# Softmax weights of a two-layer cached decode: from one permuting product and a VectorE turn to 32 small products and a ScalarE copy

## The chip, the cores and the metric

The kernel runs on one core of a Trainium2 chip. The metric is the device time of one launch in microseconds (us). Three runs of the kernel before the change took 235.09, 235.81 and 235.82 us; their median is 235.81 us. A profile was taken of one further execution, which took 235.61 us.

## The reference: what is computed

Two equal layers act on one token for each of eight batch rows (B = 8, D = 448): attention over a cache, then a small two-matrix network, each with a residual. Only the last 1024 of the 4096 cache positions are used. There are 16 query heads of 256 numbers and 8 cache heads, so two query heads share each cache head.

```python
q = (norm(x) @ wq) as 16 heads of 256
scores = q . k / 16          # per head, over W = 1024 positions
p = softmax(scores)
o = p . v
x = x + o @ wo               # 4096 -> 448
x = x + silu(norm(x) @ w1) @ w2     # 448 -> 1792 -> 448
# all of it twice; both layers use the same weights and the same cache
```

The cache dominates the memory traffic: for one batch row, 8 key slices and 8 value slices of 512 KB each, 67 MB for all eight rows. Each slice is loaded once and serves both layers.

## The kernel before, in words

**Batch rows as a pipeline.** The eight batch rows b = 0 to 7 go through the core one after the other, two of them at a time: while row b is in layer two, row b+1 is in layer one. A period of this pipeline holds, by the names that the kernel gives to its steps:

- `chain(b)`: the path with little parallel work between layer one's attention and layer two's scores: `fold1`, `xb1` (the new x in columns), `stat1`, `w1`, `yT`, `tanh`, `hT`, `w2`, `rowb2`, `fold2`, `xb2`, `x2b`, `stat2`, `wq0`/`wq1` (the new queries), `qT`, `qm`, `qd`, `qbd2`.
- scores: `S1.0` and `S1.1` (layer two of row b, key heads 0 to 3 and 4 to 7) and `S0.0`, `S0.1` (layer one of row b+1). Line 645. Each is four items of eight products; four quarters of TensorE's columns work on four key heads.
- `softmax(b, L)`, lines 654 to 676: VectorE finds the maximum (`max`, `mT`, `mg`, `mb`), ScalarE takes the exponential (`exp`, line 664), TensorE and VectorE bring the result into the form that the value products need (`perm`, line 666, and `turn`, line 668), and `l` with `rl` or `lc` makes the sums.
- values: `PVA` and `PVD` (layer one of row b+1, lines 709 and 728), `PV1.0` and `PV1.1` (layer two of row b, line 709), with ScalarE evictions `oevA.0`, `oevA.1`, `oevD`, `oev1` and small turning products `oT...`.
- `woA`, `woD` (line 781) and the eviction `rowb1` (line 1063), which feeds the next `fold1`.
- `KT0` to `KT7` (line 630): VectorE transposes each arriving key slice in its slot, two halves for each slice; a slice is scored only after that.
- `zero` (line 833): products with zeros, without use for the result.

**The change's place.** After `exp`, the exponentials E have (quarter, head) on the partitions and the 256 columns of a softmax tile in the free dimension. The value products want them the other way round, as columns of weights. Before, `perm` is one product with the constant matrix `perm` as weights and E as the moving operand (256 wide); VectorE's `turn` then transposes 32 x 32 blocks of the result into `pT_sb`.

**Loads.** SyncE issues all cache loads, in the order keys 0 to 7, values 0 to 7 for row 0, then row 1, and so on, into 30 slots used in a ring. Load n waits until load n-30 has been read for the last time. So values 6 and 7 of row b+1 wait for keys 0 and 1 of row b, which are last read by `S1.0` of row b; the keys of row b+2 wait for the rest of row b's keys and for its values. `wo` and `w2` are loaded behind row 0's keys, `w1` behind its values.

**Order.** Each task states what it reads and writes, and the program derives the waits. The order in which each engine takes its tasks is written out by hand: `ORDER` holds a string for each engine, one character for each task, which says how many of the engine's tasks not yet taken (in program order) are skipped. An engine takes its tasks strictly in that order, so a task that waits holds up everything behind it.

**Start.** VectorE's order begins with memsets of constants and of PSUM banks (`init`, `initb`, line 331), mixed with the first key transposes `KT0@0` and so on (the number behind @ is the batch row). `rsum` (lines 435 and 443) sums the columns of `w2` and `wo` on VectorE and in 20 pieces on ScalarE; `rsumd` writes the sums beside the weights, and `woD@0` needs all of those of `wo`.

Of the kernel before, what the change touches and what calls it, by code (L numbers as in the profile page):

```python
# [4 lines left out]
BF16 = mybir.dt.bfloat16  # L5
# [3 lines left out]
ACTF = mybir.ActivationFunctionType  # L9
# [5 lines left out]

ORDER = {
    "pe": (
        "000000011111l111133312223022051002010033300710500300111117777000440033333210011004403330201101044000"
        "1770000300111117777000400444423010011155510022011101044000177005000011111777700040044442320001115514"
        "0022201101044000177710000011111777700040044442320001161514002201110004400017716111101111177770004004"  # L20
        "4442320001161510022201110105400017771000001111177770004004444232000116151002201111010033001777710100"
        "ccc0b1111060000444442200011817771002022220000033ccc43a02060500001140333333300110000022220b1200000000"
        "11000"),
    "dve": (
        "pSG0G0bGq0njnwvZtutFtUEg4CQz0g4yBydzjhvHwbvnFrEAAzkayz352iuj9k6q935nikb8g14f2a4439nj90888c8685c09664"
        "4551122baaa2a929216bd1aaa10077700555555000010098880870705ac09a90087700555550000100098880870705ac09aa"
        "0077700555550000100a08880878060aab09a0087700555550000100098880870705aa0aa90077700555550000100a088808"
        "78060aab0990087700555550000100098880778060acb0b99a900005555500000000099ag90ebb8ba8006004403020100001"
        "111100000000"),
    "act": (  # L30
        "13333442444455f5e56432322224222111111113312211111111111331211111111111133122111111111113312211111111"
        "11133122100000000000220111000000000302011000000004002200010010000000"),
    "pool": (
        "00010011022002200200020002000010001000"),
}


# [164 lines left out]
def bass_interleave_layers__sliding_block_cached__dense_activation_silu__decode_kernel(  # L202
# [35 lines left out]
    perm = sb("perm", [P, P], BF16)  # L238
# [17 lines left out]
    pT_sb = [qbd[i][:, 8:264] for i in range(2)]  # L256
    E_sb = [qbd[i][:, 264:520] for i in range(2)]
# [23 lines left out]
    def QB(i, k2):  # L281
        return [("qbd", i, k2)]

    def bk(i):
        return [("bank", i)]
# [16 lines left out]
    def pe(fns, reads, writes, row, name):  # L302
        add("pe", fns, reads=reads, writes=writes, row=row, name=name)
# [63 lines left out]
    PERM = [("perm", 0), ("perm", 1)]  # L367
# [286 lines left out]
    def softmax(b, L):  # L654
        m, tb = mm[L], LB[L]
        x = bank[SC[L]][:, 0:256]
        l_ps = bank[SC[L]][:, 256:256 + H]
        dve(lambda e: e.tensor_reduce(m[:, 0:1], x, AX.X, ALU.max, negate=True), bk(SC[L]), [("mm", L)], b, "max%d" % L)  # L658
# [3 lines left out]
        dve(lambda e: e.transpose(m[:].rearrange("p (z n q) -> p z n q", z=2, q=4), view(mg[L][:], 0, [(0, 2), (1, 4), (0, 4)])),  # L662
            [("mg", L), ("mm", L)], [("mm", L)], b, "mb%d" % L)
        act(lambda e: e.activation(E_sb[L], x, ACTF.Exp, bias=m[:, 0:1], scale=1.0, accum_out=esum[:, L:L + 1]),  # L664
            bk(SC[L]) + [("mm", L)], QB(L, 1) + [("es", L)], b, "exp%d" % L)
        pe(lambda e: e.matmul(bank[tb][:, 0:256], perm[:], E_sb[L], start=True, stop=True),  # L666
           QB(L, 1) + PERM, bk(tb), b, "perm%d" % L)
        dve(lambda e: e.transpose(view(pT_sb[L], 0, [(64, 4), (1, 2), (2, 32)]),  # L668
                                  bank[tb][:, 0:256].bitcast(BF16)[:, 1:512:2].rearrange("p (u s n) -> p u s n", s=2, n=32)),
            bk(tb), QB(L, 0), b, "turn%d" % L)  # L670
# [459 lines left out]
```

## Time and profile before

| | |
|---|---|
| median of three runs | 235.81 us (235.09 to 235.82) |
| the profiled execution | 235.61 us, of which the span from first to last instruction is 233.7 us |
| busy: TensorE, VectorE, ScalarE, GpSimd | 168.2, 155.3, 68.5, 22.8 us |
| moved by DMA | 78.2 MB, nearly all in the first 35 of 40 slices |
| instructions | 8070 |

In the rows of the profile PE is TensorE (PEld its weight loads), DVE is VectorE, ACT is ScalarE, POOL is GpSimd, and SP is SyncE, which here only issues loads. A row of the timeline gives the start in us from the beginning of the span, the time it took, the engine, the line of the kernel, the operation, what it writes and reads, and how many instructions stand together in the row; in brackets stands how long the engine had been idle and what ended that. A row of a group of instructions gives the busy time, the mean duration of one in ns, and the idle time in front of them.

### The profile page before, as it was taken

How to read it: one execution, taken by the hardware profiler on the slowest of the kernel's cores; microseconds unless marked ns; L12 is line 12 of the kernel's file. 1: busy time of each engine (PE TensorE's matmuls, PEld its weight loads, DVE VectorE, ACT ScalarE, POOL GpSimd, SP SyncE). 2: the span in 40 equal slices, each digit the busy share in tenths (PEclk: the TensorE clock that was granted, in tenths of full speed). 3: DMA queues.
4: the chain of work that ended last, by engine and by line, in shares of the span. 5: the costliest groups of instructions: out<-in, count | busy, mean ns of one | idle time of the engine just before them, and what ended most of it. 6: DMA issues, size and time to landing. Idle time of an engine off the chain costs nothing.

```text
span 233.7 us, 8070 instructions
## 1 busy us (share of the span) xinstructions
PE 168.2 (72%) x3569; PEld 93.4 (40%) x3569; DVE 155.3 (66%) x412; ACT 68.5 (29%) x205; POOL 22.8 (10%) x42
## 2 busy tenths in 40 slices
PE   0001505488788888989788898889788987999873
PEld 0001503123454455446344543644464454456441
DVE  3038999986963896488578649955974795365501
ACT  2000002896222321331332233225213322333330
POOL 1000022000300200200012001101010110012000
PEclk9999999999999999999999999999999999999999
DMA  6999999999999999999999999999999998300000
GB/s 163 413 403 407 379 381 399 407 407 412 405 403 392 414 404 356 365 414 409 400 406 406 400 400 409 409 326 407 410 406 382 411 409 329 127 3 3 3 1 4
DMA packets 23401, 78.20 MB, mean 335 GB/s; under 512 B 3127, under 2 KB 6086, under 8 KB 22982
## 3 DMA queue, kind: packets, MB, share of 16 engines
q1 hardware_dynamic: 22806, 77.30, 84.7%
q8 instruction: 28, 0.46, 0.8%
q10 hardware_dynamic: 560, 0.38, 0.8%
q14 instruction: 7, 0.06, 0.1%
HBM read 77.67 MB, written 0.01 MB: 332 GB/s over the span
## 4 chain that ended last, share of the span: by engine, by line
PE 47%; DVE 22%; DMA 13%; ACT 10%; issue 5%; SPq 2%; ACTq 0%; DVEq 0%
DMA slot<-in_A_k_cache_dram 13%; PE bank L645 11%; DVE slot L630 9%; PE bank L709 7%; PE bank L872 6%; PE bank L781 4%; DVE slot L435 3%; PE bank L845 2%; ACT qbd L664 2%; PE bank L728 2%; PE bank L516 2%; ACT slot L443 2%; PE bank L885 2%; ACT qbd L698 1%; PE bank L666 1%
## 5 line engine op out<-in xcount | busy, mean ns | idle before, releaser
L630 DVE STREAM_TRANSPOSE slot<-slot 128x512 uint32<-128x512 uint32 x128 | 81.9, 682 | 16.6 <-DMA slot<-in_A_k_cache_dram 16.3
L645 PE MATMUL bank<-slot,qbd 128*16 128x256 bf16 (+1 forms) x1024 | 40.4, 286 | 7.0 <-ACT qbd L889 3.2
L645 PEld LDWEIGHTS bank<-slot,qbd 128*16 128x16 bf16 (+1 forms) x1024 | 23.9, 88 | 17.8 <-ACT qbd L889 7.2
L709 PE MATMUL bank<-slot,qbd 128*4 128x512 bf16 (+1 forms) x384 | 27.9, 388 | 1.8 <-DVE xb L584 1.3
L819 POOL TENSOR_TENSOR fcols<-fcols 128x1 f32<-128x1 f32 x17 | 9.4, 553 | 109.6 <-ACT fcols L817 109.6
L781 PE MATMUL bank<-wo_sb,q1s 128*1 128x449 bf16 x284 | 17.0, 362 | 0.4 <-ACT wo_sb L447 0.4
L872 PE MATMUL bank<-wq_sb,xbz 128*2 128x256 bf16 x512 | 16.7, 275 | 0.1
L833 PE MATMUL bank<-ident,cols 128*128 128x512 bf16 x48 | 16.2, 391 | 0.0
L620 POOL TENSOR_TENSOR qbd<-q1s,fcols 128x256 bf16<-128x256 bf16 x16 | 9.6, 612 | 65.1 <-PE bank L689 59.1
L889 ACT ACTIVATE qbd<-bank 128x256 bf16<-128x256 f32 x16 | 6.1, 383 | 32.9 <-PE bank L885 32.9
L668 DVE STREAM_TRANSPOSE qbd<-bank 128x256 bf16<-128x256 bf16 x16 | 7.7, 478 | 12.1 <-PE bank L666 11.5
L683 DVE TENSOR_TENSOR q1s<-bank,q1s 128x16 bf16<-128x16 f32 (+1 forms) x18 | 2.9, 160 | 17.7 <-PE bank L689 17.5
L698 ACT ACTIVATE qbd<-bank 128x256 bf16<-128x256 f32 x22 | 8.3, 382 | 18.4 <-PE bank L709 16.8
L709 PEld LDWEIGHTS bank<-slot,qbd 128*4 128x4 bf16 (+1 forms) x384 | 8.1, 84 | 12.6 <-issue 2.1
L536 DVE STREAM_TRANSPOSE bank<-bank 128x256 f32<-128x256 f32 (+1 forms) x25 | 10.8, 433 | 3.6 <-PE bank L1004 1.2
L872 PEld LDWEIGHTS bank<-wq_sb,xbz 128*2 128x2 bf16 x512 | 11.4, 82 | 2.8 <-DVE xbz L807 0.4
L549 PE MATMUL bank<-xb,cols 128*128 128x8 bf16 x4 | 0.3, 173 | 16.6 <-DVE cols L331 16.6
L703 ACT ACTIVATE qbd<-bank 128x512 bf16<-128x512 f32 x14 | 8.3, 595 | 11.8 <-PE bank L728 10.9
L728 PE MATMUL bank<-slot,qbd 128*12 128x512 bf16 (+3 forms) x124 | 11.2, 408 | 0.0
L658 DVE TENSOR_REDUCE mm<-bank 128x1 f32<-128x256 f32 x16 | 6.8, 423 | 6.1 <-PE bank L645 5.4
L443 ACT ACTIVATE slot<-w_sb 128x448 bf16<-128x448 bf16 x6 | 3.5, 576 | 22.3 <-DMA w_sb<-in_B_w_dram 22.2
L845 PE MATMUL bank<-w_sb,q1s 128*1 128x449 bf16 x98 | 6.5, 353 | 4.8 <-DVE q1s L827 4.8
(158 smaller groups left out, 229.9 us busy)
## 6 DMA issues: line engine op xcount, KB each, us to landing
slot<-in_A_k_cache_dram SPq DMA_DIRECT2D x64, 512.0 KB, 8.5
slot<-in_A_v_cache_dram SPq DMA_DIRECT2D x64, 512.0 KB, 11.0
wo_sb<-in_A_wo_dram SPq DMA_DIRECT2D x1, 3584.0 KB, 25.5
wq_sb<-in_A_wq_dram SPq DMA_DIRECT2D x3, 1024.0 KB, 8.7
w_sb<-in_B_w_dram SPq DMA_DIRECT2D x1, 1568.0 KB, 27.8
w_sb<-in_B_w_dram SPq DMA_DIRECT2D x1, 1344.0 KB, 17.6
wq_sb<-in_A_wq_dram SPq DMA_DIRECT2D x1, 256.0 KB, 3.6
wq_sb<-in_A_wq_dram ACTq DMA_DIRECT2D x1, 256.0 KB, 4.0
```

The costliest lines, as they stand in the source:

```text
L536: dve(lambda e: e.transpose(view(bank[bi][:], n, [(2, n // 32), (n // 16, 16), (1, 2)]), bank[bi][:, 0:n].rearrange("p (g r s) -> p g r s" ...
L620: pool(lambda e, k2=k2: e.tensor_tensor(qdata(0, k2), q1s[:, b, 64 * k2:64 * k2 + 64].rearrange("p (n r) -> p n r", r=2).unsqueeze(3) .bro ...
L630: dve(lambda e, v=v: e.transpose(v, v), SL(s, h), SL(s, h), b, "KT%d" % k)
L645: fns.append(lambda e, w=w, j=j, kv=kv, cb=cb, par=par: e.matmul(sc[32 * j:32 * j + up_to, 0:256], w, kv, start=(cb == 0 and par == 0), st ...
L698: act(lambda e, s=s: e.activation(E_sb[L], ob[:, s * DH:(s + 1) * DH], ACTF.Copy), bk(OB[L]), QB(L, 1), b, "oev%s.%d" % (name, s))
L709: return [lambda e, u=u: e.matmul(bank[OB[L] if ob is None else ob][32 * j:32 * j + 2 * n, :], pT_sb[L][:, pcol(u, c0):pcol(u, c0) + 2 * n ...
L728: pe([lambda e, t=t, c0=c0, w=w, kvh=kvh: e.matmul(bank[OB[0]][32 * t:32 * t + 2 * w, :], pT_sb[0][:, pcol(2 * t, c0):pcol(2 * t, c0) + 2 ...
L781: fns.append(lambda e, i=i, w=w, c0=c0: e.matmul(bank[XB][32 * (i % 4):32 * (i % 4) + 1, c0:c0 + D + 1], oT(i), w, start=(i < 4), stop=(i ...
L819: pool(lambda e: e.tensor_tensor(rhalf, var4, nhalf, ALU.pow), ["var4", "nhalf"], ["rhalf"], b, "pow" + name)
L833: pe(lambda e: e.matmul(bank[SC[1]][:, :], cols[:, 3:4].broadcast_to([P, P]), view(ident[:], 0, [(0, 4), (1, P)]), start=True, stop=True), ...
L845: fns.append(lambda e, f=f, w=w, c0=c0: e.matmul(bank[XB][32 * (f % 4):32 * (f % 4) + 1, c0:c0 + D + 1], hTr[b][:, f:f + 1], w, start=(f < 4),
L872: pe([lambda e, j=j, c=c, s=s, wb=wb, k2=k2: e.matmul(bank[wb][32 * j:32 * j + 2, 0:256], pair(b, xcol(c, k2), s), view(wq_sb[:], c * HD + ...
```

## The change

Three things change together.

1. `perm` becomes 32 small products. For each of the eight blocks u of 32 columns of E and each quarter q of TensorE's columns, E's block is loaded as weights (128 x 32) and 18 columns of the constant `perm` are streamed through it. The result stands in the wanted orientation already: 32 partitions for each q, 36 columns for each pair of blocks.
2. `turn` becomes one ScalarE copy (128 x 144, f32 from PSUM to bf16) in place of the VectorE transpose.
3. All four order strings are written anew.

The core of the diff:

```diff
-        pe(lambda e: e.matmul(bank[tb][:, 0:256], perm[:], E_sb[L], start=True, stop=True),
-           QB(L, 1) + PERM, bk(tb), b, "perm%d" % L)
-        dve(lambda e: e.transpose(view(pT_sb[L], 0, [(64, 4), (1, 2), (2, 32)]),
-                                  bank[tb][:, 0:256].bitcast(BF16)[:, 1:512:2].rearrange("p (u s n) -> p u s n", s=2, n=32)),
+        pe([lambda e, u=u, q=q: e.matmul(
+            view(bank[tb][32 * q:32 * q + 32, :], 36 * (u // 2) + u % 2, [(2, 18)]), E_sb[L][:, 32 * u:32 * u + 32],
+            perm[:, 32 * q:32 * q + 18], start=True, stop=True, tile_position=(0, 32 * q), skip_group_check=True)
+            for u in range(8) for q in range(4)], QB(L, 1) + PERM, bk(tb), b, "perm%d" % L)
+        act(lambda e: e.activation(view(pT_sb[L], 0, [(64, 4), (1, 36)]),
+                                   bank[tb][:, 0:144].rearrange("p (u x) -> p u x", u=4), ACTF.Copy),
             bk(tb), QB(L, 0), b, "turn%d" % L)
```

The order strings, decoded, at the places that the prediction speaks of (`x4` means four items in a row, `@3` the batch row):

```text
TensorE, one period, before:
 S1.0@3x4 S0.1@4x4 qd1@3 S1.1@3x2 perm0@4 S1.1@3x2 PVA@4x4 l0@4 oTA.0@4 xinit@4 perm1@3 l1@3 oTA.1@4 PVD@4x2
 PV1.0@3 PVD@4 PV1.0@3 PVD@4 PV1.0@3 woA@4 oTD@4 PV1.0@3 PV1.1@3 woD@4 PV1.1@3x3 fold1@4 oT1@3 zero stat1@4 w1@4
TensorE, the same period, after:
 S1.0@3x4 S0.1@4x4 qd1@3 S1.1@3x4 perm0@4 l0@4 PVA@4x4 perm1@3 l1@3 oTA.0@4 xinit@4 PV1.0@3x3 oTA.1@4 PV1.0@3
 PVD@4x4 woA@4 oTD@4 PV1.1@3x2 woD@4 PV1.1@3x2 zero fold1@4 zero oT1@3 stat1@4 w1@4
VectorE, the same period, before: max0@4 mT mg mb turn0@4 max1@3 mT mg mb rl0@4 turn1@3 oTevA@4 KT0@5 ...
VectorE, the same period, after:  max0@4 mT mg mb max1@3 mT mg mb rl0@4 oTevA@4 ...
ScalarE, the same period, before: exp0@4 oevA.0@4 exp1@3 oevA.1@4 oevD@4 lc1@3 rowb1@4 oev1@3 oTc1@3
ScalarE, the same period, after:  exp0@4 turn0@4 exp1@3 oevA.0@4 turn1@3 oevA.1@4 lc1@3 oevD@4 rowb1@4 oev1@3 oTc1@3

VectorE at the start, before: 15 memsets and small copies, KT0@0, ..., q1s rsum3 rsum3 max0@0 mT mg mb rsum2 turn0@0 ...
VectorE at the start, after:   5 memsets, KT0@0, ..., q1s KT6@0 init rsum3 rsum2 init max0@0 init mT mg x0 init inits mb ...
ScalarE at the start, before: rsum x6 exp0@0 rsum x6 oevA.0 rsum oevA.1 rsum x2 rsumd x3 rsum rsumd rsum x3 oevD rsum rsumd rowb1@0
ScalarE at the start, after:  rsum x5 exp0@0 rsum x3 turn0@0 rsum x3 rsumd rsum x2 oevA.0 rsum oevA.1 rsum x4 oevD rsum
 rsumd rsum rsumd x2 rowb1@0

VectorE in the last period, before: ... xb2@6 KT6@7 KT4@7 KT6@7 KT7@7x2 qT0@6 qm0@6 qT1@6 qm1@6 max0@7
VectorE in the last period, after:  ... xb2@6 KT4@7 KT6@7 qT0@6 KT6@7 qm0@6 KT5@7 KT7@7x2 qT1@6 qm1@6 max0@7
TensorE in the last period, before: S0.1@7x3 qd0@6 S0.1@7 S1.0@6x4 qd1@6 perm0@7 S1.1@6x4 PVA@7x4
TensorE in the last period, after:  qd0@6 S1.0@6x3 S0.1@7x4 qd1@6 S1.0@6 S1.1@6x4 perm0@7 l0@7 PVA@7x4
```

A table load on ScalarE (line 328) moves from in front of `rowb1@5` to between `x2b@2` and `var2@2`. SyncE's order, and so the order of the loads, stays as it was; GpSimd keeps its tasks in a slightly different order.

More of the change, by code (lines that the diff above doesn't have):

```diff
@@ L23 @@
-        "11000"),
-    "dve": (
[L25 to L29, printed above, removed]
+        "0000000111111111122221002201100220000440308273224012011117770680000222222000990881115100201120110220"
@@ new lines @@
+        "0066010300111117777000002233330010992077115100222021003300006660510001111777700000223333020099908111"
+        "1002201120103300006605003001111777700000223333001099908111100220112010330000666601000111177770000022"
+        "3333021099908111514002202100001100666601000111177770000022222220009990811114030220210033000066605100"
+        "011188880000002233330110bbb0111777166100122000022bbb32907105000201403333333001100000222201a091000000"
+        "20100"),
+    "dve": (
+        "1ND1s.19Bl1Alx.12xHwwfd3Fpce9aePzvkx1rlgtta57dp9p1ABg1mxxm6mejrv4f67fkdkaij6g7cc190b5883ie1605541121"
+        "52430110000088880870055909807078660044440000000888807706059a098b00666004444000000a08880870605a0c8900"
+        "96760044440000009088880770059b90a900676004444000000088880870605ca0b89006065044440000009908890770059b"
+        "0a8080766004444000000990888077005ca089080676004444000000bbj00a9g08da88000650444400200000111110000000"),
```

11 lines of the change are left out of this document (3 added, 8 removed).

## Prediction

> **What bounds the kernel now.** I read the share of the slices first, then the load issues, then one period of the timeline.
>
> ```profile
> DMA  6999999999999999999999999999999998300000
> GB/s 163 413 403 407 379 381 399 407 407 412 405 403 392 414 404 356 365 414 409 400 406 406 400 400 409 409 326 407 410 406 382 411 409 329 127 3 3 3 1 4
> ```
>
> Each digit is a slice of 5.84 us. The loads run for 34 slices and then there is a tail of about 33 us without them. While they run, most slices move 400 to 414 GB/s, a few only 326 to 382. A row of the batch needs 16 slices of 512 KB, 8.39 MB; at the 408 GB/s of the good slices that is 20.6 us. No period can be shorter.
>
> ```profile
> 67.06 0.80 SPq L456 DMA_DIRECT2D slot<-in_A_v_cache_dram  x2
> 88.58 1.64 SPq L456 DMA_DIRECT2D slot<-in_A_v_cache_dram  x2
> ...
> 173.44 1.22 SPq L456 DMA_DIRECT2D slot<-in_A_v_cache_dram  x2
> 196.34 0.80 SPq L456 DMA_DIRECT2D slot<-in_A_v_cache_dram  x2
> ```
>
> These are the issues of values 6 and 7 of rows 1, 2, 6 and 7, which wait for `S1.0` of the row before. From row 1 to row 6 five periods take 173.44 - 67.06 = 106.38 us, 21.28 each: 0.68 above what the loads need. The last takes 22.90. So the compute path sets the period, and the loads follow closely: a faster path can win 0.68 us a period at most.
>
> ```profile
> 132.83 0.61 PE L645 MATMUL bank<-slot,qbd 128*8 128x256 bf16 x16 [0.47 <-ACT qbd L889]
> 133.85 0.28 PE L666 MATMUL bank<-qbd,perm 128*128 128x256 bf16 x1 [0.41 <-ACT qbd L664]
> 134.06 0.68 PE L645 MATMUL bank<-slot,qbd 128*8 128x256 bf16 x16
> 134.17 0.49 DVE L668 STREAM_TRANSPOSE qbd<-bank 128x256 bf16<-128x256 bf16 x1 [0.98 <-PE bank L666]
> 134.78 0.42 DVE L658 TENSOR_REDUCE mm<-bank 128x1 f32<-128x256 f32 x1
> 134.81 1.03 PE L709 MATMUL bank<-slot,qbd 128*4 128x512 bf16 x16
> 136.17 0.47 ACT L664 ACTIVATE qbd<-bank,mm 128x256 bf16<-128x256 f32 x1
> 136.79 0.28 PE L666 MATMUL bank<-qbd,perm 128*128 128x256 bf16 x1 [0.20 <-ACT qbd L664]
> 137.64 0.39 PE L709 MATMUL bank<-slot,qbd 128*8 128x512 bf16 x4
> 141.79 0.28 PE L499 MATMUL bank<-cols,rowb 128*128 128x1 bf16 x5
> ```
>
> This is the softmax of one period: `S1.1`, `perm0`, the rest of `S1.1`, `turn0`, `max1`, `PVA`, `exp1`, `perm1`, the first `PV1.0`, and `fold1` at its end. VectorE stands still for 0.98 us in front of `turn0`, and only behind it may it take `max1`.
>
> **The change part by part.** *The 32 products.*
>
> ```profile
> 203.53 0.55 PE L740 MATMUL bank<-qbd,slot 128*128 128x32 bf16 x16
> 229.09 0.86 PE L1013 MATMUL bank<-w_sb,q1s 128*1 128x112 bf16 x56 [0.53 <-DVE q1s L827]
> L740 PE MATMUL bank<-qbd,slot x16: 176/176/176, 203.5 to 203.9; 128*128 128x32 bf16 x16
> L1013 PE MATMUL bank<-w_sb,q1s x56: 210/211/213, 229.1 to 229.7; 128*1 128x112 bf16 x56
> ```
>
> No row shows 32-column weights in four quarters. Narrow products over the whole array follow each other every (0.55 - 0.176)/15 = 0.025 us. In four quarters, 56 products make 14 groups: (0.86 - 0.21)/13 = 0.05 us for a group of four, with 112 columns to stream. At 18 columns a group should come near the 0.025. So eight groups take 0.2 us if the quarters load side by side, and 32 x 0.025 = 0.8 us if they load one after the other. I take 0.2, the quartered row being the nearest in kind; with 0.18 for the last product to end, `perm` takes 0.38 in place of the 0.28 us shown above. The ends are 0 (eight groups at 12 ns) and +0.7.
>
> The Trainium skill, "TensorE: Matmul & The Clock Gate", section "Wait — 56ns, not 53.3ns?", says that the starts of two products never lie closer than about 25 ns, however narrow they are. By it the 32 take 0.8 us. The quartered row above, 12 ns a product, does not agree.
>
> *The copy.*
>
> ```profile
> L1008 ACT ACTIVATE slot<-bank 128x112 f32<-128x112 f32 x1 | 0.3, 255 | 0.0
> L698 ACT ACTIVATE qbd<-bank 128x256 bf16<-128x256 f32 x22 | 8.3, 382 | 18.4 <-PE bank L709 16.8 <-PE bank L728 1.3 <-PE bank L689 0.3
> L668 DVE STREAM_TRANSPOSE qbd<-bank 128x256 bf16<-128x256 bf16 x16 | 7.7, 478 | 12.1 <-PE bank L666 11.5 <-PE bank L773 0.6
> ```
>
> Between 112 and 256 columns, 144 take 0.255 + 32/144 x 0.127 = 0.28 us on ScalarE, against 0.48 on VectorE. `perm` and `turn` together change by +0.1 - 0.2 = -0.1 us. ScalarE takes on 16 x 0.28 = 4.5 us; behind the copy in its order stand `exp1` and then `oevA.0`. VectorE is rid of 7.7 us of work and up to 12.1 of standing still.
>
> *A period with the new orders*, walked through on the rows above. `S1.1` runs in one piece, 132.83 to about 133.9; `perm0` starts when `exp0` is done, 133.85, and ends near 134.25; the copy ends at 134.6; `PVA` starts at 134.65 (-0.15). `max1` starts at 133.95 instead of 134.78, so `exp1` is ready at 135.1; its products stand behind `PVA` on TensorE, 135.75; their copy stands behind `oevA.0` on ScalarE and ends near 136.5, and `PV1.0` starts at 136.55 instead of 137.64. From there the same products follow in another order, with `woD` behind half of `PV1.1`; `fold1` comes at about 141.45 (-0.35). `oT1` then waits less in front of `stat1`, and `w1` gains 0.6. `wq0` now goes ahead of `stat2` in most rows, which starts TensorE earlier, but `qm0` then waits for the later `var2`; I count nothing. So the path offers 0.6 of the possible 0.68 us.
>
> ```profile
> DVE slot L630 <- DMA slot<-in_A_k_cache_dram: 16.3, 5, 12.2
> ```
>
> I take 0.4 of it. What is late next is a key slice: `KT0` of the next row waits for its load already (16.3 us in all, 12.2 of them at the start), and the new order puts both halves of `KT0@6` and `KT0@7`, and one of `KT0@3` and `KT0@4`, in front of `oTevD`, which `woD` needs. Five periods: -2.0 (ends 0 and -3.4).
>
> *The start.*
>
> ```profile
> 0.92 0.48 DVE L331 MEMSET bank<- 128x512 f32 x1 [0.92 <-PEq L1115]
> ...
> 3.10 0.18 DVE L331 MEMSET fcols<- 32x1 f32 x3
> 15.49 0.71 DVE L630 STREAM_TRANSPOSE slot<-slot 128x512 uint32<-128x512 uint32 x1 [12.21 <-DMA slot<-in_A_k_cache_dram]
> 36.27 0.69 DVE L608 CAST q1s<-bank 128x512 bf16<-128x512 f32 x1 [0.36 <-PE bank L600]
> 36.88 5.80 DVE L435 TENSOR_REDUCE slot<-wo_sb 128x6 f32<-128x2688 bf16 x2
> 39.10 0.58 ACT L443 ACTIVATE slot<-w_sb 128x448 bf16<-128x448 bf16 x1 [22.16 <-DMA w_sb<-in_B_w_dram]
> 39.80 0.58 ACT L443 ACTIVATE slot<-w_sb 128x448 bf16<-128x448 bf16 x1
> 43.74 0.47 ACT L664 ACTIVATE qbd<-bank,mm 128x256 bf16<-128x256 f32 x1 [0.47 <-DVE mm L662]
> 53.03 1.45 PE L781 MATMUL bank<-wo_sb,q1s 128*1 128x449 bf16 x16
> 55.46 0.93 PE L781 MATMUL bank<-wo_sb,q1s 128*1 128x449 bf16 x16 [0.41 <-ACT wo_sb L447]
> 56.45 0.55 ACT L1063 ACTIVATE rowb<-bank 128x450 bf16<-128x450 f32 x1 [1.13 <-PE bank L781]
> ```
>
> VectorE blocks at the first key transpose until 15.49. Before, 15 small tasks lie ahead of it in the idle time, from 0.92 to 3.28, with 2.1 us of work; after, 5 (0.4 us). The other 1.7 us now follow 15.49, while one half of `KT6` (0.6) and some memsets move behind `q1s`. Net, `q1s` comes about 0.4 us later. Between it and `exp0@0` then stand `KT6`, a short in place of a long sum, and five small tasks: another 0.55. `exp0@0` starts near 44.7.
>
> ScalarE's sums start at 39.10 whatever the order (they wait for `w2`) and cost 0.70 each. Five of them end at 42.6, and ScalarE stands still until 44.7: 2.1 us instead of 0.5. After `exp0@0` it has 15 sums (10.5), the copy (0.3), `oevA.0`, `oevA.1` and `oevD` (1.3), four `rsumd` (0.5) and `exp0` itself (0.6): 44.7 + 13.2 = 57.9 for the last `rsumd`. Now `woD@0` waits for it: 0.95 us later, near 59.0, comes `rowb1@0`, in place of 56.45. That is +2.6 us, and nothing covers it: behind `rowb1` come `fold1@0`, `chain(0)`, `S1.0@0`, and with it the issue at 67.06. TensorE also waits nearly 3 us in front of `woD@0`; the two `wo` rows show the same 16 products at 1.45 and 0.93 us, so some products in `chain(0)` would take the slow pace: +0.3 (ends 0 and 1). Start: +2.9 (ends +1.8 and +4).
>
> *The rest.*
>
> ```profile
> 190.41 3.07 DVE L630 STREAM_TRANSPOSE slot<-slot 128x512 uint32<-128x512 uint32 x5
> 193.41 0.42 DVE L536 STREAM_TRANSPOSE bank<-bank 128x256 f32<-128x256 f32 x1
> 160.56 1.28 ACT L328 ACT_TABLE_LOAD   x1
> 219.77 0.28 PE L666 MATMUL bank<-qbd,perm 128*128 128x256 bf16 x1 [0.95 <-ACT qbd L664]
> 220.61 0.39 PE L709 MATMUL bank<-slot,qbd 128*4 128x512 bf16 x4
> ```
>
> In the last period `qT0@6` stood behind five key transposes until 193.41; now it stands ahead of three of them, and `S1.0@6` can start 1.2 us earlier. But `S0.1@7` and `exp0@7` move behind `S1.0@6`, which gives 1.05 back before `PVA@7`: -0.15. The table load, hidden before, now delays `var2@2`; about 0.3 reaches `qm0@2`: +0.3. In the tail only `perm1@7` and its copy change: -0.1. No load is added, and the loads keep their order. The sum, against the profiled execution's 235.61: +2.9 - 2.0 - 0.15 + 0.3 - 0.1 = +0.95, so **236.6 us**; the median of the runs lies 0.2 above that execution, which I leave out.
>
> **The rivals.** *The debt is paid back (other side).* If the period falls to 20.65, five periods win 3.2 instead of 2.0, and with a start at +2.0 and no slow products the sum is about -1.2 to -1.7: 234.2. The place is the stretch from `max1` to `fold1`; it decides from 0.6 us a period on. For it speak the standing still in front of `turn0`; against it the key loads, which would have to keep their full rate without a dip. *The start costs nothing.* Should the key slices or `w2` land at other times, or ScalarE catch up, the gain stands alone: -2.0 to -3.2, about 232.8. Against it: the row at 39.10 depends on a load that does not change. *The quarters do not overlap.* Then each `perm` takes 0.6 us more, of which about 0.45 lies on the path: the period keeps its 21.28, and the start and the tail pay too: 235.61 + 2.9 + 0.3 + 0.5 = 239.3. Against it: the quartered row's 12 ns a product. The Trainium skill's 25 ns ("TensorE: Matmul & The Clock Gate", the section named above) would bring this rival about.
>
> **How the numbers follow.** Likeliest, the start not wholly paid back: 0.45, from 235 to 238. Paid back: 0.32. No debt: 0.11. No overlap: 0.12. Of the first I count a quarter as within 0.3% (0.7 us, about what a measurement of this kernel can tell from no change), of the second a tenth. Faster: 0.29 + 0.11 = 0.40; within: 0.14; slower: 0.34 + 0.12 = 0.46. The range, 232.8 to 239.2, reaches to the other cases.
>
> **What would show it.** Each `perm` group: eight groups, first start to last end 0.38 us. The copy: 0.28 us. `exp0@0` near 44.7, `rowb1@0` near 59.0, the first issue of values 6 and 7 of row 1 near 70. The same issues from row 1 to row 6 spaced 20.9 us. VectorE's busy time falls to about 148 us. Wrong would make it: `rowb1@0` before 57.5, or a spacing at 20.6 or above 21.3.

## The result and the profile after

The changed kernel takes 242.88 us (median of four executions, 241.81 to 244.43) against 235.81 us before: a ratio of 1.031, 95% interval 1.024 to 1.037. Forecast were 236.6 us and a range up to 239.2, so the kernel is slower by far more than the forecast allowed. The profiled execution took 241.81 us, its span is 240.0 us: 6.3 us longer than the span before. Executions of later runs that took over 1.5% more than the fastest of their kernel, at a lower granted clock, are left out of the figures below.

The share of the slices and the rate of the loads, from the page of the changed kernel; a slice is now 6.0 us:

```profile
DMA  6999999999999998999999599999999999600000
GB/s 164 406 408 406 379 381 403 407 408 409 406 341 395 412 407 270 391 412 393 401 402 416 203 328 411 410 350 411 405 406 315 380 412 375 203 3 3 3 4 3
```

Before, the lowest slice within the loads was 326 GB/s. Now there are slices at 270, 203 and 315: the loads, which wait for free slots, were issued later than the DMA engines could have taken them. The issues of values 6 and 7 of rows 1 to 7, from the timeline of the changed kernel (start, duration, queue, line):

```profile
68.76 0.80 SPq L455 DMA_DIRECT2D slot<-in_A_v_cache_dram  x2
90.79 1.23 SPq L455 DMA_DIRECT2D slot<-in_A_v_cache_dram  x2
112.43 0.80 SPq L455 DMA_DIRECT2D slot<-in_A_v_cache_dram  x2
137.43 0.81 SPq L455 DMA_DIRECT2D slot<-in_A_v_cache_dram  x2
159.00 0.80 SPq L455 DMA_DIRECT2D slot<-in_A_v_cache_dram  x2
180.58 1.68 SPq L455 DMA_DIRECT2D slot<-in_A_v_cache_dram  x2
204.19 1.73 SPq L455 DMA_DIRECT2D slot<-in_A_v_cache_dram  x2
```

The first stands 1.70 us later than before (67.06). The next five periods take 22.03, 21.64, 25.00, 21.57 and 21.58 us, 111.82 in all against 106.38. The last takes 23.61 against 22.90, and from its end to the end of the span it is 35.8 us against 37.4. So +1.7 + 5.4 + 0.7 - 1.6 = 6.2 us: 5.4 us lie in the five periods that were to win 2.0, and 3.7 of these in a single one.

One ordinary period shows that the new operations themselves are what was forecast. Row 4's softmax in the changed kernel, from its timeline (idle time in front and its releaser in brackets):

```profile
139.11 1.08 PE L644 MATMUL bank<-slot,qbd 128*8 128x256 bf16 x32 [0.47 <-ACT qbd L890]
140.13 0.38 PE L665 MATMUL bank<-perm,qbd 128*32 128x18 bf16 x32
140.24 0.42 DVE L657 TENSOR_REDUCE mm<-bank 128x1 f32<-128x256 f32 x1 [0.76 <-PE bank L644]
140.62 0.29 ACT L669 ACTIVATE qbd<-bank 128x144 bf16<-128x144 f32 x1 [0.54 <-PE bank L665]
141.06 1.03 PE L710 MATMUL bank<-slot,qbd 128*4 128x512 bf16 x16 [0.22 <-ACT qbd L669]
141.39 0.47 ACT L663 ACTIVATE qbd<-bank,mm 128x256 bf16<-128x256 f32 x1 [0.48 <-DVE mm L661]
142.84 0.82 PE L710 MATMUL bank<-slot,qbd 128*8 128x512 bf16 x12
143.84 0.17 DVE L684 TENSOR_TENSOR q1s<-bank,q1s 128x16 bf16<-128x16 f32 x1 [2.34 <-PE bank L690]
146.31 0.35 PE L782 MATMUL bank<-wo_sb,q1s 128*1 128x449 bf16 x1
146.88 0.93 PE L782 MATMUL bank<-wo_sb,q1s 128*1 128x449 bf16 x15 [0.22 <-issue]
148.46 0.28 PE L498 MATMUL bank<-cols,rowb 128*128 128x1 bf16 x5
```

The 32 products take 0.38 us, the copy 0.29. Counted from the start of `S1.1`, `PV1.0` comes at 3.73 us where it came at 4.81 before: the gain of 1.1 us is there, to a few hundredths. But `fold1` comes at 9.35 instead of 8.96. One cause stands in the row at 146.88: of the 16 products of `woD` the first starts at 146.31, and then TensorE stands still until 146.88 while it waits for nothing that the profile shows ("issue").

Such rows of the changed kernel, with the one in front of the largest:

```profile
100.86 0.74 PE L782 MATMUL bank<-wo_sb,q1s 128*1 128x449 bf16 x12 [0.23 <-issue]
118.53 0.60 PE L710 MATMUL bank<-slot,qbd 128*8 128x512 bf16 x5
120.36 0.60 PE L710 MATMUL bank<-slot,qbd 128*8 128x512 bf16 x7 [1.24 <-issue]
190.05 0.35 PE L782 MATMUL bank<-wo_sb,q1s 128*1 128x449 bf16 x2 [0.93 <-issue]
```

At 118.74 us TensorE stops in the middle of `PV1.0` and goes on at 120.36; this is the period of 25.00 us. The period is 3.4 us longer than the ones beside it, so more was lost than the stop of 1.6. The windows of the timeline, each as long as the shortest stretch of the clock's record (3.41 us); behind the engines' busy times stand the granted clock, the DMA share and GB/s:

```profile
117.54:120.95 3.41, 1.96 (x56) 0.91 (x52) 0.00 (x0) 1.01 (x3) 0.00 (x0) 1.00 1.04 414
120.95:124.37 3.42, 3.42 (x41) 1.10 (x38) 0.79 (x2) 0.67 (x2) 0.00 (x0) 0.50 1.03 410
124.37:127.78 3.41, 3.19 (x57) 1.36 (x49) 2.89 (x7) 1.22 (x3) 0.61 (x1) 1.00 1.02 396
```

After a window with 1.96 us of products the clock is granted at half for one window. That isn't needed for the loss, though: two of the four executions had a mean granted clock of 1.000 and took 242.3 and 243.4 us.

### The profile page after: what moved, and what is told of

The parts are those of the page before. It is cut to its first block, busy times and chain, and to the rows that moved or that the text cites. A ratio compares the mean times of both kernels' runs of the same rounds, so it can differ in the third digit from the quotient of the medians.

```text
span 240.0 us, 9059 instructions
## 1 busy us (share of the span) xinstructions
PE 172.6 (72%) x4065; PEld 97.1 (40%) x4065; DVE 149.5 (62%) x396; ACT 73.4 (31%) x221; POOL 22.7 (9%) x42
## 4 chain that ended last, share of the span: by engine, by line
PE 58%; DVE 16%; ACT 11%; issue 6%; DMA 5%; POOL 2%; SPq 1%; DVEq 0%; ACTq 0%
PE bank L644 12%; PE bank L710 10%; PE bank L782 7%; DVE slot L629 7%; DMA slot<-in_A_k_cache_dram 5%; PE bank L873 4%; PE bank L729 4%; PE bank L515 3%; ACT slot L442 2%; PE bank L846 2%; PE bank L690 2%; PE bank L886 2%; PE bank L834 2%; PE bank L665 2%; ACT qbd L890 2%
## 5 line engine op out<-in xcount | busy, mean ns | idle before, releaser
L644 PE MATMUL bank<-slot,qbd 128*16 128x256 bf16 (+1 forms) x1024 | 38.6, 285 | 8.6 <-ACT qbd L890 4.7
L710 PE MATMUL bank<-slot,qbd 128*4 128x512 bf16 (+1 forms) x384 | 29.5, 391 | 3.9 <-ACT qbd L669 2.2
L644 PEld LDWEIGHTS bank<-slot,qbd 128*16 128x16 bf16 (+1 forms) x1024 | 23.3, 88 | 18.4 <-ACT qbd L890 7.6
L684 DVE TENSOR_TENSOR q1s<-bank,q1s 128x16 bf16<-128x16 f32 (+1 forms) x18 | 3.1, 174 | 32.3 <-PE bank L690 32.2
L782 PE MATMUL bank<-wo_sb,q1s 128*1 128x449 bf16 x284 | 18.6, 376 | 1.8 <-issue 1.4
L710 PEld LDWEIGHTS bank<-slot,qbd 128*4 128x4 bf16 (+1 forms) x384 | 7.5, 84 | 11.2 <-issue 4.3
L782 PEld LDWEIGHTS bank<-wo_sb,q1s 128*1 128x1 bf16 x284 | 6.7, 86 | 11.5 <-issue 4.2
L663 ACT ACTIVATE qbd<-bank,mm 128x256 bf16<-128x256 f32 x16 | 7.6, 474 | 11.5 <-DVE mm L661 11.5
L588 PE MATMUL bank<-slot,wq_sb 128*128 128x16 bf16 x128 | 3.6, 174 | 8.0 <-DVE slot L581 8.0
```

The lines of the kernel that those rows point to most:

```text
L644: fns.append(lambda e, w=w, j=j, kv=kv, cb=cb, par=par: e.matmul(sc[32 * j:32 * j + up_to, 0:256], w, kv, start=(cb == 0 and par == 0), st ...
L710: return [lambda e, u=u: e.matmul(bank[OB[L] if ob is None else ob][32 * j:32 * j + 2 * n, :], pT_sb[L][:, pcol(u, c0):pcol(u, c0) + 2 * n ...
L782: fns.append(lambda e, i=i, w=w, c0=c0: e.matmul(bank[XB][32 * (i % 4):32 * (i % 4) + 1, c0:c0 + D + 1], oT(i), w, start=(i < 4), stop=(i ...
```

## The experiments

All ratios are to the kernel before, run on the same chip; its medians there were 235.85 to 236.37 us.

### Which part costs: operations or orders

*The new operations with the orders of before.* The order strings are those of before, with `turn` moved into ScalarE's.

```diff
 ScalarE, one period
- exp0@4 oevA.0@4 exp1@3 oevA.1@4 oevD@4
+ exp0@4 turn0@4 oevA.0@4 exp1@3 oevA.1@4 turn1@3 oevD@4
```

> The 32 products and the ScalarE copy, with the order strings of before (turn0 behind exp0, turn1 behind oevA.1 on ScalarE). Theory A (the loss has three parts: the longer start, wq0 ahead of stat2 in five rows, and TensorE standing still for its own instructions, of which there are 992 products and their weight loads more): 237 to 239 us, rows of TensorE with idle time put down to issue, 31 or 32 instruction packets instead of 28. Theory B (only the orders cost, the new operations are free): 235 to 236 us. Theory C (the new operations cost nearly all, the new orders gain): 241 us or more.

(992 is the number of instructions: 496 products and as many weight loads.) Measured: 248.06 us, 1.054 (1.050 to 1.058). The operations alone cost 12 us, more than the whole change; of the three theories only C allowed for that much, and its gain by the new orders is tested further below. The profile has 32 instruction packets, and these rows with the most issue:

```profile
78.63 0.74 PE L782 MATMUL bank<-wo_sb,q1s 128*1 128x449 bf16 x11 [1.84 <-issue]
116.91 0.27 PE L886 MATMUL bank<-qm,spread 128*128 128x64 bf16 x2 [0.92 <-issue]
123.44 0.82 PE L729 MATMUL bank<-slot,qbd 128*16 128x512 bf16 x9 [1.31 <-issue]
163.68 0.49 PE L644 MATMUL bank<-slot,qbd 128*8 128x256 bf16 x9 [1.04 <-issue]
169.66 0.20 PE L665 MATMUL bank<-perm,qbd 128*32 128x18 bf16 x4 [0.42 <-issue]
```

None but the last stands at the new products: TensorE stops in `woD`, `qd`, `PVD` and the scores.

*The new orders with the operations of before.*

```diff
 VectorE, one period (single permuting product, turn on VectorE)
- max0@4 mT mg mb max1@3 mT mg mb rl0@4 oTevA@4
+ max0@4 mT mg mb turn0@4 max1@3 mT mg mb rl0@4 turn1@3 oTevA@4
```

> The new orders with the single permuting product and the VectorE turn (turn0 in front of max1, turn1 behind rl0). Theory A: 238 to 239.5 us: +1.7 from the start, +0.4 in each of the five rows with wq0 ahead of stat2, no idle time of TensorE put down to issue beyond that of before. Theory B: 242 to 243.5 us, as the changed kernel. Theory C: 235 us or less.

Measured: 242.47 and 244.69 us, 1.028 and 1.037 times the 235.88 of the kernel before. No theory had this. The profile (242.47 us) has one row of issue above 0.3 us, and that one not at a block end as explained below, so this is another loss: `S1.0` of row 0 starts at 69.3 us instead of 67.6 in the changed kernel, and `exp1` comes 0.6 us later than there, since `max1` waits behind the turn. The first five periods take 110.5 us in all, against 106.4 before. The new orders need the copy.

### Is it the number of instructions?

*8 of the 32 products.* Everything else as in the changed kernel.

```diff
-            for u in range(8) for q in range(4)], QB(L, 1) + PERM, bk(tb), b, "perm%d" % L)
+            for u in range(8) for q in range(1)], QB(L, 1) + PERM, bk(tb), b, "perm%d" % L)
```

> The changed kernel with only the products of the first quarter: 8 in place of 32, so three quarters of the layer weights are left out and the result is not that of the reference; everything else is as in the changed kernel. If TensorE stands still for its instructions (theory A), the 768 instructions fewer take that away: 28 or 29 instruction packets, almost no idle time put down to issue, 239.5 to 241 us. If the stalls are hidden by the loads or have another cause: 242.5 to 243.5 us.

Measured: 237.24 us, 1.006 (1.003 to 1.009): 5.6 us less than the changed kernel, more than was expected. The eight still take 0.37 us where the 32 take 0.38, so it isn't their own duration that went.

*The same number of instructions elsewhere.* In the kernel before, two of the useless `zero` products in each group are cut into 32.

```diff
-            pe(lambda e: e.matmul(bank[SC[1]][:, :], cols[:, 3:4].broadcast_to([P, P]), ...), ..., "zero")
+            pe([lambda e, u=u, q=q: e.matmul(
+                bank[SC[1]][32 * q:32 * q + 32, 18 * u:18 * u + 18], cols[:, 3:4].broadcast_to([P, 32]),
+                ident[:, 18 * q:18 * q + 18], start=True, stop=True, tile_position=(0, 32 * q), skip_group_check=True)
+                for u in range(8) for q in range(4)] if i < 2 else [...], ..., "zero")
```

> The kernel before, with two of the zero products of each row cut into 32 quartered products of 18 columns each, which take about as long together: 496 products, 992 instructions of TensorE more, as in the changed kernel, but away from the softmax and with no other change. If the number of TensorE's instructions is what costs (theory A): 32 instruction packets in place of 28, several idle stretches of TensorE of 0.3 to 2 us put down to issue, and 239 to 248 us. Rival (the price lies in the softmax: quartered products there, or the copy): 235.5 to 236.5 us.

Eighteen `zero` products were cut in fact, so 558 products and 1116 instructions were added (9186 in place of 8070). The 32 pieces take 0.37 to 0.41 us together, a whole `zero` product 0.39. Measured: 248.31 us, 1.052 (1.048 to 1.056). Without any change to softmax or orders the kernel loses 12.5 us. Five of its rows with issue:

```profile
69.39 0.74 PE L645 MATMUL bank<-slot,qbd 128*8 128x256 bf16 x19 [1.46 <-issue]
108.01 0.20 PE L499 MATMUL bank<-cols,rowb 128*128 128x1 bf16 x2 [0.56 <-issue]
115.08 1.08 PE L645 MATMUL bank<-slot,qbd 128*8 128x256 bf16 x29 [1.87 <-issue]
154.73 0.40 PE L645 MATMUL bank<-slot,qbd 128*16 128x256 bf16 x7 [1.20 <-issue]
162.18 1.33 PE L645 MATMUL bank<-slot,qbd 128*16 128x256 bf16 x39 [2.11 <-issue]
```

So the number of TensorE's instructions is what costs. The traces also show where. I counted all of TensorE's recorded instructions from 1 on, in the order of their starts (products, weight loads, and some 50 that only wait or signal), and numbered the packets of its instruction queue (16 KB each) from 0. Every stop put down to issue of 0.5 us and more in the changed kernel, in the operations with the old orders and in the padded kernel lies between instruction 256 j + 449 and the next, behind packet j. The four of the changed kernel (us):

```text
packet j   packet landed   instruction 256j+449 starts   the next starts   stop
   8          99.44               100.28                    100.86         0.58
  11         118.77               118.74                    120.36         1.61
  15         145.55               146.31                    146.88         0.57
  22         188.59               188.76                    190.05         1.28
```

TensorE comes to the end of a block of 256 instructions, and goes on 1.3 to 1.6 us after the next block's packet has landed. How late the packets are, by the same count: from instruction 256 j + 193, where the block in front of the late one begins, to the start of packet j it takes 2.8 to 5.2 us (3.6 in the mean) while the loads run in the kernel before, and 0.4 us in the mean in the tail without loads. With 1.0 us for the packet and about 1.4 behind it, a block must last some 6 us; this is an estimate from these means. Under the loads blocks lasted 7.0 us in the mean before, the shortest 5.3; in the changed kernel it is 6.3 and 4.4. That a packet is asked for where the block in front of it begins is my assumption; the rest is read off.

The stops don't make up the whole loss. Under the loads, those above 0.15 us add up, from one start to the next, to 4.4 us in the changed kernel, 8.4 with the old orders and 12.2 in the padded kernel; the losses are 7.0, 12.2 and 12.5 us. The kernel before already has 1.4 us of such stops, none above 0.43. How the rest comes about (the half clock, or tasks and loads that come later behind a stop) wasn't divided up.

*Do the packets wait behind the loads?* The first attempt halved the value slices by partitions, from row 2 on, with the new operations and old orders:

```diff
-        dma(lambda e: e.dma_start(slots[s][:, :]..., cache[b, kvh, S0:SK, :].rearrange("(p u) d -> p u d", p=P)),
+        np = P // 2 if cache is A_v_cache and b > 1 else P
+        dma(lambda e: e.dma_start(slots[s][0:np, :]..., cache[b, kvh, S0:SK, :].rearrange("(p u) d -> p u d", p=P)[0:np]),
```

> The 32 products and the copy in the orders of before, and from row 2 on only half of each value slice is loaded (the other half keeps old data, so the result is not the reference's): the instructions stay, the loads leave room. Theory A1 (TensorE's instructions come late because their packets wait behind the cache loads): no idle time put down to issue from about 95 us on, periods of 21.2 us or less from there, 238 to 241 us (the stall of the second row, with full loads, stays). Theory A2 (the sequencer can't feed so many instructions, whatever the loads do): the same stalls, 246 to 248 us.

Measured: 253.61 and 257.10 us, 1.082 (1.074 to 1.090). The profile, of an execution of 259.11 us, has stops of up to 3.65 us. The loads had no more room than before: they moved 194 to 324 GB/s at a DMA share of 0.93 to 1.04. The run answers nothing about room, only that slower loads and longer stops came together. The second attempt takes half of each partition's run instead, which was to relieve all DMA engines, and does the same to the kernel before as a control:

```diff
+        nu = 4 if cache is A_v_cache and b > 1 else 8
+        dma(lambda e: e.dma_start(slots[s][:, :].rearrange("p (u d) -> p u d", d=DH)[:, 0:nu, :],
+                                  cache[b, kvh, S0:SK, :].rearrange("(p u) d -> p u d", p=P)[:, 0:nu, :]),
```

> The 32 products and the copy in the orders of before; from row 2 on only the first half of each partition's run of the value slices is loaded (2 KB of 4 KB on all 128 partitions; the rest keeps old data, so the result is not the reference's). The loads then have room on all DMA engines. Theory A1 (TensorE's instructions come late because their packets wait behind the loads): from about 100 us on no idle time put down to issue above 0.3 us, and at most 4 us above before_short_values (the stall of the second row stays). Theory A2 (the number of instructions alone): the stalls stay, 8 us or more above before_short_values.

> The kernel before with the same shortened loads from row 2 on (the result is not the reference's): the control for ops_short_values, and the measure of how far the loads set the period before. If the computing path sets it: 234.5 to 236 us. If the loads held it back by what they can at most, 0.6 us a period: 232 to 234 us.

Measured: 241.35 us, 1.021 (1.015 to 1.026), and for the control 235.51 us, 0.996 (0.994 to 0.998). All rows with issue of the first (its profiled execution took 242.52 us):

```profile
66.16 0.42 PE L645 MATMUL bank<-slot,qbd 128*16 128x256 bf16 x8 [0.16 <-issue]
77.99 1.16 PE L783 MATMUL bank<-wo_sb,q1s 128*1 128x449 bf16 x11 [0.97 <-issue]
```

From row 2 on, with the same 32 packets, there is none, and the packets start 2.3 us behind the mark of the count above in the mean, against 3.9 us with full loads. The difference of 5.8 us is above the 4 that was expected: 4.9 of it stand already at `S1.0` of row 1 (93.27 against 88.41 us, after a later start and the stop at 78 us, under full loads). The rest of the run to `S1.0` of row 7 takes 129.75 against 127.24 us; what makes these 2.5 us isn't shown. So the instructions come late because of the loads. The control says a second thing: with room for the loads the kernel before wins only about 0.4%. Its period is set by the computing path, as the prediction read it.

### What orders and copy are worth without the extra instructions

One of the 32 products is kept, so TensorE has as many instructions as before.

```diff
-            for u in range(8) for q in range(4)], QB(L, 1) + PERM, bk(tb), b, "perm%d" % L)
+            for u in range(1) for q in range(1)], QB(L, 1) + PERM, bk(tb), b, "perm%d" % L)
```

> The changed kernel with 1 of the 32 products (the other 31 left out, so the result is not the reference's): as many instructions of TensorE as before, with the new orders and the copy. Theory A (instructions make the loss; copy and orders are worth little together): 235 to 237 us, 28 instruction packets. Rival (the orders cost as well, 2 us or more): 238 us and above.

> The orders of before (turn0 behind exp0, turn1 behind oevA.1 on ScalarE), the copy, and 1 of the 32 products (the other 31 left out, so the result is not the reference's): the copy in place of the VectorE turn, and nothing else. Theory A: 235 to 236.5 us. Rival (the copy on ScalarE holds back what stands behind it): 238 us and above.

Measured: new orders 235.86 us, 0.999 (0.996 to 1.002); old orders 235.79 us, 0.997 (0.995 to 1.000). Orders and copy together are worth nothing that can be told from zero. A last point between: 8 products in the old orders.

> The new operations with 8 of the 32 products (the other 24 left out, so the result is not the reference's) and the copy, in the orders of before (turn0 behind exp0, turn1 behind oevA.1). Against the run with the 32 products in these orders it shows what the 24 products cost. Theory A (the count of instructions is the whole price of the new operations): 234.5 to 236.5 us, 29 instruction packets, at most one idle stretch put down to issue. Rival (the copy and its place on ScalarE cost too): 239 us or more.

Measured: 240.32 us, 1.017 (1.013 to 1.022), above what was expected; its profile has a stop of 1.36 us by issue at 115.34. In the middle row of the table the orders so differ by 3 us, at some 220 instructions more than in the first (instructions rounded):

```text
products of a softmax   instructions   packets   new orders   old orders
        1                  8070          28        235.86       235.79 us
        8                  8290          29        237.24       240.32 us
       32                  9060          32        242.88       248.06 us
```

### Two orders looked at singly

In the changed kernel, TensorE takes `wq0` ahead of `stat2` in five rows, and `S1.0` came 1.0 to 1.5 us behind the end of `wq1` there, against 0.8 before. I took that for a cause, and put `stat2` back.

```diff
 TensorE, rows 0, 1, 2, 4, 5
- wq0 stat2 wq1
+ stat2 wq0 wq1
```

> The changed kernel with stat2 back in front of wq0 in rows 0, 1, 2, 4 and 5. Theory A: from the end of wq1 to S1.0 it takes 0.8 us in these rows instead of 1.2 to 1.4, and the time falls by 1.5 to 2.5, to about 241 us. Rival (the loads or the stalls set the period, and the chain only shares in them): no change, 242.5 to 243.5 us.

> Eight products a softmax (the other 24 left out, so the result is not the reference's) and stat2 back in front of wq0 in rows 0, 1, 2, 4 and 5. Without the stalls the order's own price must show: theory A, 0.4 us less in each of these rows, about 235.4 us (234.8 to 236.3) against the 237.2 of eight products alone. Rival (the loads set the period, the chain's end is hidden): 237 us.

> As eight_stat2 (the other 24 products left out), and the orders of VectorE, ScalarE and TensorE up to rowb1@0 taken from before. Theory A (the new start costs 1.4 to 1.7 us): 233.8 us (233 to 234.8), rowb1@0 1 to 2 us earlier. Rival (the start was late because its first key slice landed late): as eight_stat2.

Measured: with all 32 products 247.93 us, 1.052 (1.044 to 1.059); with eight, 238.19 us, 1.009 (1.007 to 1.012); with eight and the old start, 237.27 us, 1.007 (1.004 to 1.010). The theory falls. From the end of `wq1` to `S1.0` it did shrink to 0.8 us, but of the five rows only in rows 1 and 4 (with the old start in row 4 alone); and `wq0` now waits for `stat2`, and `wq1` ends later: with eight products `S1.0` of row 4 comes 21.16 and 20.89 us after that of row 3 in the two runs, against 20.97 without the edit. And with 32 products the same instructions in another order cost 5 us more: block ends fell into other places, with stops of 0.98, 1.60, 1.14, 1.69 and 1.42 us (8.0 us in all by the sum above, against 4.4). The start's worth, 0.002 between the last two ratios, lies within their intervals.

### Two tries for a faster version

*Two products in place of 32*, of 128 columns of E each, with the values loaded in 1 KB runs, the scores' moving operand read position by position, and the orders of the run with eight products and the old start. The diff is without the values' loads.

```diff
-                        "p (u cb jj par) -> p cb par u jj", u=8, cb=4, par=2)[:, cb, par, :, :]
+                        "p (u cb jj par) -> p cb par jj u", u=8, cb=4, par=2)[:, cb, par, :, :]
...
+            view(bank[tb][:], v, [(36, 4), (2, 18)]), E_sb[L][:, v:256:2],
+            view(perm[:], 0, [(32, 4), (1, 18)]), start=True, stop=True, skip_group_check=True)
+            for v in range(2)], QB(L, 1) + PERM, bk(tb), b, "perm%d" % L)
```

> The whole computation with 2 products a softmax, of 128 columns of E as weights and 72 streamed columns, in place of 32 in quarters: the value slices are loaded in another layout (1 KB runs instead of 4 KB), and the scores are streamed in the order of the positions. Orders and start as in eight_stat2_start. If the instructions were the price and nothing else changes: 233 to 235 us, 27 or 28 instruction packets, no idle time put down to issue. If 1 KB runs load more slowly or the scores' products take longer than 0.61 us for eight: 238 us or more, and the GB/s row or the scores' row shows it.

Measured: 332.27 us. The group of the scores' products (count, busy us, mean ns):

```profile
L649 PE MATMUL bank<-slot,qbd 128*16 128x256 bf16 (+1 forms) x1024 | 141.9, 687 | 6.8 <-ACT qbd L895 4.7 <-POOL qbd L624 2.0
```

A product took 687 ns instead of 285, though it reads the same 256 columns: in the new reading order neighbours lie 512 bytes apart. The 1 KB runs cost as well: where they follow each other, value slices landed 1.49 us apart, key slices in 4 KB runs 1.28. With that a row's loads need 8 x 1.28 + 8 x 1.49 = 22.2 us, so this way was given up.

*The late value products first*, in the kernel before; `exp1` and `turn1` move back on ScalarE and VectorE accordingly:

```diff
 TensorE, one period
- oTA.0@4 xinit@4 perm1@3 l1@3 oTA.1@4 PVD@4x2 PV1.0@3 PVD@4 PV1.0@3 PVD@4 PV1.0@3 woA@4 oTD@4 PV1.0@3 PV1.1@3 woD@4 PV1.1@3x3 fold1@4
+ oTA.0@4 xinit@4 oTA.1@4 PVD@4x3 perm1@3 l1@3 PVD@4 woA@4 oTD@4 PV1.0@3x3 woD@4 PV1.0@3 PV1.1@3x4 fold1@4
```

> The kernel before with its own operations and instructions, and one part of the orders new: in periods 1 to 6 the late value products of layer one (PVD) go ahead of perm1 and of layer two's values, exp1 behind oevA.1, turn1 behind oTevA. If fold1 and the end of PV1.1 both come 0.4 us earlier and the loads allow it: 233 to 234.5 us. If layer two's values, now later, end later and hold back stat1, or the loads set the period: 235.5 to 237 us.

Measured: 239.35 us, 1.014 (1.010 to 1.017). `PVD` ends hardly earlier (8.6 to 9.0 us after `S1.0`, before 8.7 to 9.4), `PV1.0` starts some 1.9 us later in most periods, and `fold1`, now behind all of `PV1.1`, comes 0.3 us later in the mean. Part of the loss can be block ends: their stops add up to 3.0 us here, with 28 packets, against 1.4 before. No version beat the kernel before.

## Why the prediction was wrong

**The 32 products: right by the clock, wrong by the bill.** Forecast were 0.38 us for `perm`, 0.28 for the copy. Measured were 0.38 and 0.29, in these groups of the changed kernel:

```profile
L665 PE MATMUL bank<-perm,qbd 128*32 128x18 bf16 x512 | 6.1, 181 | 3.5 <-ACT qbd L663 3.5
L669 ACT ACTIVATE qbd<-bank 128x144 bf16<-128x144 f32 x16 | 4.6, 290 | 3.9 <-PE bank L665 3.8
L684 DVE TENSOR_TENSOR q1s<-bank,q1s 128x16 bf16<-128x16 f32 (+1 forms) x18 | 3.1, 174 | 32.3 <-PE bank L690 32.2
```

From the first product to the last end it is 0.38 us, so with 0.18 for the last one 31 starts lie within 0.20 us, 6.5 ns apart. They stand in eight groups of four, one product for each quarter, 25 ns from group to group, as the prediction put it. The quarters overlap; the rival without overlap falls. The step that failed is the sentence "`perm` and `turn` together change by +0.1 - 0.2 = -0.1 us". It priced the time in which 32 products run, and not that TensorE must be fed 62 more instructions a softmax, 992 in all. Those cost 242.88 - 235.86 = 7.0 us, the difference between the changed kernel and the same with one product. Part of that can be the one product's shorter time (0.19 us); between 8 and 32 products, whose times are 0.37 and 0.38 us, it is 5.6 us. All the rest of the forecast, +0.95 us, comes out at -0.5 us by the run with one product (235.86 against 236.37 us on that chip, interval -1.0 to +0.5). The profile of the kernel before held the hint unread: its line of the instruction queue (28 packets), 8070 instructions, and at block ends the small stops counted above, the longest 0.43 us. How near the limit was shows only in that count, not in a row.

The Trainium skill, "Runtime: NRT & Kernel Launch", section "Instruction fetch mechanics", states that an engine's instructions come in blocks of 256 through a DMA queue of its own, while the block before is executed, and that crossing a block is mostly hidden. The blocks of 256 are what the traces show. That it is mostly hidden holds for the kernel before (stops of 1.4 us in all) and for the tail; under full loads and with blocks shorter than about 6 us it does not hold here.

**The period with the new orders: -2.0 forecast, not found.** The walk was right up to `PV1.0` (forecast 1.1 us earlier, measured 1.08) and for `exp1` (from the start of `S1.1`, 2.28 us instead of 3.34). It failed at "`fold1` comes at about 141.45 (-0.35)". With one product, five periods take 108.4 us (from `S1.0` of row 0 to that of row 5: 176.42 - 68.05) against 106.4, and `fold1` comes 12.3 us after `S1.0` in their mean, against 12.0. This profiled execution took 237.05 us, 1.2 above the run's median, and 2.5 of the 108.4 us are stops at block ends, against 0.5 of the 106.4. With eight products the five periods take 107.1 us, 0.3 of them stops. By none of these counts is there a gain. Two things seem to have kept it; neither was tested by a run of its own with the new orders. First, `PVD` ends where it did (8.72 us after `S1.0` of row 3, before and after), since the new order puts three items of `PV1.0` in front of it. Second, VectorE's standing still moved, in large part, rather than went. Against the last row above stands this one of the kernel before:

```profile
L683 DVE TENSOR_TENSOR q1s<-bank,q1s 128x16 bf16<-128x16 f32 (+1 forms) x18 | 2.9, 160 | 17.7 <-PE bank L689 17.5
```

In front of the evictions `oTevA` and `oTevD` VectorE waits 32.3 us instead of 17.7 (25.1 with one product); in front of the turn it had waited 12.1. Its idle time in a period rose from 5.6 to 6.4 us before to 6.5 to 7.3 (eight products), and behind it the key transposes are late: in periods 0, 2 and 4 `S0.1` ends 0.3 to 0.9 us later after `S1.0` than before. "What is late next is a key slice" was right in kind, and its price was set too low.

**The start: +2.9 forecast, +1.7 measured.** From the timeline of the changed kernel:

```profile
45.21 0.47 ACT L663 ACTIVATE qbd<-bank,mm 128x256 bf16<-128x256 f32 x1 [2.54 <-DVE mm L661]
54.46 1.67 PE L782 MATMUL bank<-wo_sb,q1s 128*1 128x449 bf16 x16
57.16 0.93 PE L782 MATMUL bank<-wo_sb,q1s 128*1 128x449 bf16 x16 [0.39 <-DVE slot L629]
58.15 0.55 ACT L1064 ACTIVATE rowb<-bank 128x450 bf16<-128x450 f32 x1 [1.13 <-PE bank L782]
```

`exp0@0` came at 45.21 (forecast 44.7), 0.33 of it because the first key slice was transposed at 15.82 instead of 15.49. `rowb1@0` came at 58.15 (forecast 59.0). The step "44.7 + 13.2 = 57.9" was too large: from 45.21 the last sum's division ended 11.8 us later, at 57.02. Each sum was priced at the 0.70 us between two starts, but where a short task stands between two sums it fills part of that spacing. The slow products came in `woA` (1.67 us), `woD` ran at full pace.

**The rest**, by the same profiled execution with one product. In the last period the forecast was -0.15. Measured are 20.59 us against 22.90, and the next stretch 21.20 against 20.27: -1.4, since `S1.0@6` no longer waits for `qT0` behind five key transposes and its cost in front of `PVA@7` was overrated. The tail from `S1.0@7` was forecast at -0.1; the last result is ready 14.7 us after it, 14.9 before, and what follows is 1.1 us shorter, which isn't explained. That the sum without the instructions came near the forecast is luck: these gains of 1.4 and 1.1 us, of which 0.25 was forecast, stand against the missing ones in the periods. VectorE's busy time in the changed kernel fell to 149.5 us (forecast 148).

Of the rivals, none had the mechanism. The one that came nearest in time, 239.3 us, had the price of the 32 products, but as their duration.

## What to carry to other kernels

Count instructions as a resource of its own. Where TensorE runs 256 of them (products and weight loads together) in less than about 6 us (the estimate above) while the DMA queues are full of loads, it can stop at block ends, for 0.5 to 2 us each in these runs, wherever those happen to fall; cutting one product into many small ones costs there, however short they are. Look at the rows of idle time with no releaser and the count of instruction packets before and after, and price an edit at equal instruction count first; a new order alone also moves the block ends. And an engine's idle time that an order takes away in one place is won only if what it does next is ready: here it stood in front of the next wait.

## What the runs showed of the hardware

- A stop of TensorE for instructions ends 1.3 to 1.6 us after the block's packet has landed, in the changed kernel and in the kernels with 32 products or padding. The packet itself takes 1.0 us in the mean.
- A lower clock doesn't need a whole idle window: after 1.96 us of products in 3.41 us the next 3.41 us were granted 0.50, in the padded kernel after 1.44. Where the limit lies isn't shown: with the new operations and old orders a window with 1.56 us of products, from 76.32 us on, was followed by the full clock. The Trainium skill, "TensorE: Matmul & The Clock Gate", section "What's actually happening", has the same window of 3413 ns, and asks for an idle window; these weren't idle throughout.
- The moving operand's reading order counts: 687 ns instead of 285 for 256 columns when neighbours lie 512 bytes apart.
- Loading half the partitions of a slice didn't relieve the queues: 194 to 324 GB/s at a DMA share of 0.93 to 1.04; loading half of each partition's run did in part (two windows of 10 us, from 130 and 150 us on, at 0.60 and 0.63).
